# Moving the first batch's imaginary-part transfers, row tiles 0 and 1, from SyncE's DMA queue to GpSimd's

## The chip, the cores and the metric

The kernel runs on one core of a Trainium2 chip. The metric is the device time of one execution in microseconds (us), lower is better. The core has TensorE (PE, with its weight loads PEld), VectorE (DVE), ScalarE (ACT), GpSimd (POOL) and SyncE (SP). SP only issues transfers here; POOL issues transfers and does small copies. Transfers of either queue are carried by the same 16 DMA engines.

## The reference

Three stages follow each other. The first is a recurrence over time for 4 batches, 8 heads, 768 steps and a head width of 48; two MLP blocks work on its output.

```
S_re, S_im = 0
for t in range(S):
    new_re = ar * S_re - ai * S_im
    new_im = ar * S_im + ai * S_re
    S_re, S_im = new_re + k[t] v[t]^T, new_im
    y[t] = q[t] @ S_re
x = heads of y side by side              # B, S, 384
x = token mixing and channel MLP of x    # w_tok1, w_tok2, w_ch1, w_ch2
out = x + MLP(normalised x)              # g_ln, w_ch1, w_ch2
```

`ar` and `ai` are the complex decay, scaled to a magnitude of at most 0.999.

## The kernel before

The decay of a step is written as a magnitude and an angle, so that the recurrence becomes a product over time chunks of 128 steps: q and k are scaled by cumulated magnitudes and turned by cumulated angles. The turned vectors have a real part (times the cosine) and an imaginary part (times the sine). For one head both parts are stacked on 96 partitions of one tile, `stk`: rows 0 to 47 real, 48 to 95 imaginary. TensorE then works on a head with that one tile.

The elementwise work (generator `gen_E`, class `Piece`) does not go by heads. It goes by row tiles of 128 rows (head times width): a batch has 384 rows, so three row tiles i = 0, 1, 2, and in the first batch each is done in two halves `hf` of 384 time steps. Row tile 0 holds heads 0 and 1 and the first 32 rows of head 2; row tile 1 the last 16 rows of head 2, heads 3 and 4, and 16 rows of head 5; row tile 2 the rest. The steps of a piece are F, G (magnitudes and their cumulated product), H (scale q and k), T1, T2 (angles, sine, cosine) and T3.

T3 (line 318 on) does the product with the cosine into the piece's scratch `self.R` (DVE, line 173 is the helper that issues it) and the product with the sine in place into `qkt` (the tile `qk`). Then it copies, row range by row range, the real part (line 342, out of `t`, `u` or `w` in the profile's names, which are the scratch tiles) and the imaginary part (line 343, mostly out of `qk`) into the head's `stk`. In the first batch heads 2 to 7 use tiles with the tag `w2`, so the profile writes `w` for their `stk`. Row tile 0 gives 3 row ranges in each half, row tile 1 gives 4: 6 and 8 transfers of imaginary parts. The last real-part transfer of a row tile is kept as `fin["stk", i]`; the load of the next batch's decay (line 59, 768 KB) is issued after it.

TensorE's work on the heads is in `gen_P`: transposes of k (line 524), scores (line 538), filler matmuls `warm` (line 462), the chunk sums (line 566, which need `kT`, evacuated by ACT in line 526), a scan over the chunks on DVE (line 567), and the output (lines 586 and 598). DVE masks the scores (line 544).

The weights come as 64-bit words and are split on DVE and ACT (`split_w`, lines 632 to 648). `load_raw` (line 615) loads them: pieces 0 to 2 on SP's queue, the others on POOL's. POOL's queue also stores two split pieces early on (`tokw_d`, line 668).

The order of instructions is made in two steps. The Python code yields between generators by budgets (`run_E`, `run_P`, `run_W`), which gives the order in the program; then a planner built into the framework simulates a timeline and orders the instructions on each engine by which are ready first. On the chip each engine and each queue works strictly in that order and waits on semaphores.

`DQ` (line 1213) is empty in the kernel before, so the choice in line 343 always falls on SP:

```
last_dma = nc.sync.dma_start(out=stk[b, h][d0:d0 + m, hf], in_=self.R[r:r + m, k])
(nc.gpsimd if (b, i) in DQ else nc.sync).dma_start(out=stk[b, h][D + d0:D + d0 + m, hf], in_=qkt[r:r + m, k])
```

Of the kernel before, what the change touches and what calls it, by code (L numbers as in the profile page):

```python
# [17 lines left out]
B, H, S, D = 4, 8, 768, 48  # L18
# [4 lines left out]
FT = 1536 // P  # L23
# [15 lines left out]
def tile_kernel(ctx: ExitStack, tc: tile.TileContext, a_in, qk_in, v_in, aq2_in, v2_in, wt_in, wm1_in, wm2_in, w64_in, g_in, c_in, out):  # L39
# [41 lines left out]
    vstat = cp.tile([P, 2 * B], F32, name="vstat")  # L81
    n_q = 3 * len(YS) + 3 * len(QZ)
    qstat = cp.tile([P, max(n_q, 1)], F32, name="qstat")
# [28 lines left out]
    def tmp():  # L112
        return ap.tile([P, HB], F32, tag="r", name="r", bufs=NR)
# [42 lines left out]
    hscan = {}  # L156
# [29 lines left out]
    def after(key):  # L186
        return tc.issue_after(fin[key]) if key in fin else ExitStack()
# [15 lines left out]
    class Piece:  # L203
# [21 lines left out]
        def F(self):  # L225
# [4 lines left out]
            yield "wait"  # L230
            with tc.issue_after(tab["ops"][-1]) if b and GSQ else ExitStack():
                A.activation(out=self.sq.rearrange("p (x s) -> p x s", x=2), in_=self.both, func=AF.Square)  # L232
# [231 lines left out]
    def gen_P(alt):  # L464
# [22 lines left out]
        def evac(y, h, n):  # L487
            yv = y[:, 0:NCH * D].rearrange("p (c e) -> p c e", c=NCH)
            dst = slice(h * D, (h + 1) * D)
            scale = US / (VS * SS) if n in YS else US  # L490
            A.activation(out=xh[:, :, dst], in_=yv, func=AF.Copy, scale=scale)
            V.scalar_tensor_tensor(out=xl[:, :, dst], in0=yv, scalar=scale, in1=xh[:, :, dst], op0=ALU.mult, op1=ALU.subtract)
            A.activation(out=junk_p, in_=yv, func=AF.Square, scale=scale, accum_out=ustat[:, n:n + 1])

        for n, (b, h) in enumerate(heads):
# [3 lines left out]
            def qc(c, x):  # L499
                return kq[:, c // 3, x * HB + (c % 3) * P:x * HB + (c % 3 + 1) * P]  # L500
# [20 lines left out]
            for half in range(2):  # L521
                if half == 0:
                    for c in range(5):
                        T.transpose(tr[:, c * 96:(c + 1) * 96], qc(c, 1), eye[0:96, 0:96])  # L524
                    with after(AHOLD.get(n)):
                      kTc = A.activation(out=kT, in_=tr[:, 0:480].rearrange("p (c d) -> p c d", c=5), func=AF.Copy, scale=(VS * SS if n in YS else 1.0) / (QS if n in QZ else 1.0))
                    if n in YS:
                        vh = ap.tile([P, S], F32, tag="dw", name="vh", bufs=NDW).bitcast(F16)
                        Uh = vh[0:2 * D, 2 * NCH * D:4 * NCH * D].rearrange("p (x c e) -> p x c e", x=2, c=NCH)
                        Uc = U.rearrange("p e c -> p c e")  # L530
                        vh = vh[:, 0:2 * NCH * D].rearrange("p (x c e) -> p x c e", x=2, c=NCH)
                        m = YS.index(n)
                        A.activation(out=vh[:, 0], in_=v, func=AF.Copy, scale=VS)
# [3 lines left out]
                for c in range(3 * half, 3 * half + 3):  # L537
                    last = T.matmul(sc[:, (c % 3) * P:(c % 3 + 1) * P], qc(c, 1), qc(c, 0), start=True, stop=True)  # L538
                if n in YS or b == 0 and h % 2 < SR:
                    sT.append(tmp().rearrange("p (c t) -> p c t", c=3))  # L540
# [23 lines left out]
                if half == 1:  # L564
                    for c in range(5):
                        T.matmul(Gv.rearrange("p (e c) -> p e c", c=NCH)[:, :, c], kT[:, c], v[:, c], start=True, stop=True)  # L566
                    scan = V.tensor_tensor_scan(out=U.rearrange("p e c -> p (e c)"), data0=Gv, data1=dr.rearrange("p e c -> p (e c)"), initial=0.0, op0=ALU.add, op1=ALU.mult)
# [29 lines left out]
                elif c:  # L597
                    T.matmul(yc, qc(c, 0), U[:, :, c - 1], start=False, stop=True)
            late = (lambda y=y, h=h, n=n: evac(y, h, n))
            if h == H - 1 or not LATE:  # L600
                late()
                late = None
            yield ("done", b, h)
# [7 lines left out]
    def load_raw(n, tag):  # L611

        raw = ap.tile([P, 2, 2 * HB + 3], F32, tag="w2", name="raw", bufs=6).rearrange("p a b -> p (a b)")[:, 0:2 * S].bitcast(I32) if tag == "w2" else ap.tile([P, 2 * S], I32, tag="tw", name="raw", bufs=NTW)
        with after(("pc", 0, RG, 1) if RG >= 0 and 4 <= n < 6 else None):
          (nc.sync if n < NSY else nc.gpsimd).dma_start(out=raw.bitcast(U8), in_=w_src[n].bitcast(U8)[:, 3:3 + 8 * S])  # L615
        return raw

    def load_w(n):
        while len(raws) <= n:
            m = len(raws)  # L620
            raws[m] = load_raw(m, "w2" if m in RW2 else "tw")

    def split_w(dst, n):

        load_w(min(27, AHEAD(n)))
        if not pad:
            pad.append(ap.tile([P, S], U32, tag="pad", name="pad", bufs=1) if PADB else ap.tile([P, S], U32, tag="dw", name="pad", bufs=NDW))
            G.memset(pad[0], 0.0)
        raw = raws[n]
        byte = raw.bitcast(U8).rearrange("p (a b) -> p a b", b=8)[:, :, 4]  # L630
        y = raw.rearrange("p (a b) -> p a b", b=2)[:, :, 0]
        V.scalar_tensor_tensor(out=pad[0].bitcast(U8).rearrange("p (a b) -> p a b", b=4)[:, :, 3], in0=byte, scalar=3, in1=byte, op0=ALU.logical_shift_left, op1=ALU.bitwise_and)  # L632
        V.scalar_tensor_tensor(out=y.bitcast(U32), in0=y.bitcast(U32), scalar=5, in1=pad[0], op0=ALU.logical_shift_right, op1=ALU.bitwise_or)
        w = y.bitcast(F32).rearrange("p (i s) -> p i s", i=2)
        wact[n] = A.activation(out=dst[:, :, 0], in_=w, func=AF.Copy, scale=WS).ins
        if NW0 <= n < NW1:
            if not eye_w:
                eye_w.append(ap.tile([P, P], F32, name="eye_w"))
                eye_w.append(ap.tile([P, P], F16, name="eye_m"))
                A.activation(out=eye_w[0], in_=eye, func=AF.Copy, scale=WS)  # L640
                A.activation(out=eye_w[1], in_=eye, func=AF.Copy, scale=-1.0)
            for i in range(2):
                p = psum("y", 1)[:, 0:HB]
                T.matmul(p, eye_w[0], w[:, i], start=True, stop=False)
                T.matmul(p, eye_w[1], dst[:, i, 0], start=False, stop=True)
                A.activation(out=dst[:, i, 1], in_=p, func=AF.Copy)
            return
        wop[n] = V.scalar_tensor_tensor(out=dst[:, :, 1], in0=w, scalar=WS, in1=dst[:, :, 0], op0=ALU.mult, op1=ALU.subtract).ins
# [14 lines left out]
    def gen_W():  # L663
        for n in range(4):
            hl = wm1[STG + n]
            with after("scan"):
                split_w(hl, n)
            nc.gpsimd.dma_start(out=tokw_d[n // 2, :, n % 2], in_=hl)
            yield 0
        for j, wm in enumerate((wm1, wm2)):  # L670
            for n in range(FT):
                if j and n % 2 == 0:
                    w = ap.tile([P, 2, 2 * HB + 3], F32, tag="w2", name="w2", bufs=6).rearrange("p a b -> p (a b)")
                    for i in range(2):
                        wm2[n + i] = w[:, i * 2 * DM:(i + 1) * 2 * DM].bitcast(F16).rearrange("p (a b c) -> p a b c", a=2, b=2)
                with (tc.issue_after(hscan[WGH]) if 4 + j * FT + n >= WGN and j == 0 else after('r1') if 4 + j * FT + n >= WGR and j == 0 else ExitStack()):
                    split_w(wm[n], 4 + j * FT + n)
                yield j * FT + n + 1

# [364 lines left out]

    st = {"phase": "", "alt": True, "e": 0, "p": 0, "pp": 0, "w": 0, "need": 0, "bb": 0, "c": 0, "mk": 0}
    E, Pg, Wg, M = gen_E(), gen_P(lambda: st["alt"]), gen_W(), gen_M()

    e0 = []
# [69 lines left out]
    def check_next():  # L1118
        n = st["c"]
        if n >= 2:  # L1120
            check_w(n - 2)
        if n < 28:
            again[n] = load_raw(n, "tw")
        st["c"] += 1
# [20 lines left out]
    for b in range(B):  # L1145
        k = 0
        st["bb"] = b
        while True:
# [21 lines left out]
            for _ in range(2):  # L1170
                n = st["p"]
# [34 lines left out]
LATE = 1  # L1206
# [6 lines left out]
DQ = ()  # L1213
# [3 lines left out]
FE = 0  # L1217
LQ = 0
RG = -1
GSQ = 1  # L1220
PIPE = 0
IV = 0
WGN, WGR, WGH = 99, 99, 7
# [43 lines left out]
EW = 2  # L1267
LQ = 1
RG = 1
YS = [n for n in range(32) if n >= YH or n in YX]  # L1270
QZ = [n for n in range(32) if n >= QH or n in YX]
_INS = ["a", "qk", "v", "aq2", "v2", "wt", "wm1", "wm2", "w64", "g", "c"]
# [49 lines left out]
```

## Time and profile before

| | us |
|---|---|
| median of 3 runs | 899.06 |
| lowest, highest | 897.23, 906.02 |
| the profiled execution | 897.11 |
| its span, first to last instruction | 895.0 |
| PE busy (share of the span) | 802.0 (90%) |
| DVE, ACT, POOL busy | 630.4, 603.4, 93.5 |

The profiled execution is 2.1 us longer than its span. Times in the rows below count from the start of the span. A timeline row gives start, duration, engine, line, operation, output and inputs, and, in square brackets, how long the engine had been idle and what released it. "SPq" is SP's queue; the duration there is the time of issuing. A transfer lands later; the views of transfers give the time from issue to landing.

### The profile page before, as it was taken

What the parts mean: (1) busy time and instruction counts of PE and PEld (TensorE: products, weight loads), DVE (VectorE), ACT (ScalarE), POOL (GpSimd) and SP (SyncE); (2) the same over time, 40 slices, a digit from 0 to 9 for tenths busy, and PEclk for the clock granted to TensorE, in tenths of its full rate; (3) what the DMA queues carried; (4) which work ended last, traced back from release to release, by engine and by line L of the source; (5) the groups of instructions that cost most, each with busy time, mean ns of one, the idle gap of its engine ahead of it and who ended that gap; (6) DMA issues with size and microseconds to landing.
All of it is one profiled execution on the core that took longest, in us unless ns stands there. A gap on an engine that the chain in (4) does not pass through costs nothing.

```text
span 895.0 us, 15729 instructions
## 1 busy us (share of the span) xinstructions
PE 802.0 (90%) x5802; PEld 543.0 (61%) x5802; DVE 630.4 (70%) x1094; ACT 603.4 (67%) x1631; POOL 93.5 (10%) x171
## 2 busy tenths in 40 slices
PE   0089898999989898899999999999999999999996
PEld 0078785555757676456766666566666656656563
DVE  6797469999988799776898885956565332455443
ACT  8787248675668798984999984985665423454542
POOL 0311010311001010210030010100000000011110
PEclk9977979999999999999999999999999999999998
DMA  8355684255742715410421614131010111566662
GB/s 306 86 163 156 200 298 141 57 156 168 227 140 61 208 53 172 136 55 27 116 74 34 173 39 131 45 83 34 12 50 21 34 63 37 174 205 187 201 218 96
DMA packets 41604, 108.26 MB, mean 121 GB/s; under 512 B 5904, under 2 KB 23824, under 8 KB 41520
## 3 DMA queue, kind: packets, MB, share of 16 engines
q1 hardware_dynamic: 31936, 56.72, 21.3%
q0 software_dynamic: 9584, 50.47, 17.1%
q8 instruction: 47, 0.77, 0.4%
q14 instruction: 37, 0.30, 0.1%
HBM read 77.20 MB, written 11.01 MB: 99 GB/s over the span
## 4 chain that ended last, share of the span: by engine, by line
PE 44%; ACT 8%; DVE 5%; DMA 2%; issue 0%; SPq 0%; DVEq 0%; ACTq 0%
PE m L683 13%; PE m L682 13%; PE m L684 13%; ACT t L200 2%; DMA stk<-t 1%; PE sc L538 1%; ACT hid L690 1%; PE tr L566 1%; DVE t L173 1%; DVE hid L692 1%; ACT junk L745 0%; DVE xc L800 0%; DVE qk L173 0%; PE tr L817 0%; PE tr L524 0%
## 5 line engine op out<-in xcount | busy, mean ns | idle before, releaser
L692 DVE SCALAR_TENSOR_TENSOR hid<-m,hid 128x384 f16<-128x384 f32 x198 | 109.2, 553 | 131.9 <-ACT hid L690 131.5
L682 PE MATMUL m<-u,w 128*128 128x384 f16 x576 | 187.7, 326 | 6.4 <-DVE u L742 3.2
L684 PE MATMUL m<-u,w 128*128 128x384 f16 x576 | 187.7, 326 | 0.0
L683 PE MATMUL m<-u,w 128*128 128x384 f16 x576 | 187.7, 326 | 0.0
L683 PE MATMUL m<-hid,w 128*128 128x384 f16 x540 | 175.6, 326 | 4.8 <-DVE hid L692 4.5
L684 PE MATMUL m<-hid,w 128*128 128x384 f16 x540 | 175.5, 326 | 0.0
L690 ACT ACTIVATE hid<-m 128x384 f16<-128x384 f32 x198 | 95.3, 481 | 118.5 <-PE m L684 117.8
L684 PEld LDWEIGHTS <-w 128*128 128x128 f16 x1176 | 115.1, 98 | 81.9 <-issue 12.2
L683 PEld LDWEIGHTS <-w 128*128 128x128 f16 x1176 | 115.4, 98 | 79.0 <-issue 8.7
L682 PEld LDWEIGHTS <-w 128*128 128x128 f16 x1176 | 114.5, 98 | 79.2 <-issue 12.5
L682 PE MATMUL m<-hid,w 128*128 128x384 f16 x540 | 128.9, 326 | 9.3 <-ACT hid L690 9.2
L173 DVE SCALAR_TENSOR_TENSOR t<-t 128x384 f32<-128x384 f32 x80 | 44.2, 554 | 21.5 <-ACT t L232 14.0
L538 PE MATMUL sc<-stk 96*128 96x128 f32 x300 | 44.3, 282 | 1.4 <-DVE r L544 1.4
L661 ACT ACTIVATE sq<-sq 128x768 f16<-128x768 uint8 x28 | 23.6, 843 | 28.3 <-DVE sq L660 28.3
L615 POOL DMA_DIRECT2D raw<-in_wm x48 | 25.6, 534 | 162.0 <-DVE sq L660 83.0
L538 PEld LDWEIGHTS sc<-stk 96*128 96x128 f32 x300 | 40.0, 194 | 3.7 <-DVE r L544 1.7
L200 ACT ACTIVATE t<-t 128x384 f32<-128x384 f32 x80 | 40.9, 514 | 0.5 <-DVE t L173 0.3
L524 PE MATMUL m<-cst,stk 96*128 96x96 f32 x10 | 1.7, 291 | 43.2 <-DMA stk<-qk 43.2
L690 ACT ACTIVATION_READ_ACCUMULATOR hid<-m 128x1 f32 x198 | 38.6, 195 | 0.0
L173 DVE TENSOR_TENSOR qk<-qk,t 128x768 f32<-128x768 f32 x40 | 38.0, 951 | 0.4
L198 ACT ACT_TABLE_LOAD x27 | 34.6, 1283 | 1.3 <-PEq L1314 0.9
L632 DVE SCALAR_TENSOR_TENSOR pad<-raw 128x768 uint8<-128x768 uint8 x28 | 28.8, 1029 | 9.0 <-DMA raw<-in_wt 6.1
(281 smaller groups left out, 1689.0 us busy)
## 6 DMA issues: line engine op xcount, KB each, us to landing
raw<-in_wm POOLq DMA_DIRECT2D x48, 768.0 KB, 4.9
qk<-in_qk SPq DMA_DIRECT2D x23, 384.0 KB, 4.0
aj<-in_a SPq DMA_DIRECT2D x9, 768.0 KB, 5.0
stk<-t SPq DMA_DIRECT2D x40, 144.6 KB, 3.1
stk<-qk SPq DMA_DIRECT2D x40, 144.6 KB, 3.1
raw<-in_wt SPq DMA_DIRECT2D x6, 768.0 KB, 5.9
v<-in_v SPq DMA_DIRECT2D x32, 144.0 KB, 2.3
x_d<-xc SPq DMA_DIRECT2D x24, 192.0 KB, 2.8
```

Source lines behind the costliest of these rows:

```text
L173: r = getattr(nc.vector, n)(*a, **k)
L198: tab.update(set=s, load=A.preload_act_table_set(sets[s]).ins, ops=[])
L200: tab["ops"].append(A.activation(**k).ins)
L538: last = T.matmul(sc[:, (c % 3) * P:(c % 3 + 1) * P], qc(c, 1), qc(c, 0), start=True, stop=True)
L615: (nc.sync if n < NSY else nc.gpsimd).dma_start(out=raw.bitcast(U8), in_=w_src[n].bitcast(U8)[:, 3:3 + 8 * S])
L632: V.scalar_tensor_tensor(out=pad[0].bitcast(U8).rearrange("p (a b) -> p a b", b=4)[:, :, 3], in0=byte, scalar=3, in1=byte, op0=ALU.logical ...
L661: A.activation(out=t[:, HB:2 * HB].bitcast(F16), in_=bad_, func=AF.Copy, accum_out=wstat[:, n:n + 1])
L682: T.matmul(out_, wh, xh_, start=first, stop=False)
L683: T.matmul(out_, wh, xl_, start=False, stop=False)
L684: T.matmul(out_, wl, xh_, start=False, stop=last)
L690: A.activation(out=hl[:, 0], in_=p, func=AF.Relu, accum_out=hstat[:, n_h[0]:n_h[0] + 1])
L692: last[:] = [V.scalar_tensor_tensor(out=hl[:, 1], in0=p, scalar=0.0, in1=hl[:, 0], op0=ALU.max, op1=ALU.subtract).ins]
```

## The change

`DQ` becomes `((0,0),(0,1))`: in batch 0, the imaginary-part transfers of row tiles 0 and 1 (14 transfers) are issued from GpSimd's queue. Real parts, row tile 2 and the batches 1 to 3 stay on SP.

The diff also adds three names whose values leave the rest as it was: `EV` is empty, `WH` is empty (so `WH.get(n, "scan")` is `"scan"`), and `RGN` is `(4, 5)`, which is the old `4 <= n < 6`.

```diff
-            if h == H - 1 or not LATE:
+            if h == H - 1 or not LATE or n in EV:
...
-        with after(("pc", 0, RG, 1) if RG >= 0 and 4 <= n < 6 else None):
+        with after(("pc", 0, RG, 1) if RG >= 0 and n in RGN else None):
...
-            with after("scan"):
+            with after(WH.get(n, "scan")):
...
-                with (tc.issue_after(hscan[WGH]) if 4 + j * FT + n >= WGN and j == 0 else after('r1') if 4 + j * FT + n >= WGR and j == 0 else ExitStack()):
+                with after(WH[4 + n]) if j == 0 and 4 + n in WH else (tc.issue_after(hscan[WGH]) if 4 + j * FT + n >= WGN and j == 0 else after('r1') if 4 + j * FT + n >= WGR and j == 0 else ExitStack()):
...
+RGN = (4, 5)
+WH = {}
+EV = ()
...
+DQ = ((0,0),(0,1))
```

## Rows read from the trace of the kernel before

**Rows 1.** The page: span and the first engine's busy time.
```profile
span 895.0 us, 15729 instructions
...
PE 802.0 (90%) x5802; PEld 543.0 (61%) x5802; DVE 630.4 (70%) x1094; ACT 603.4 (67%) x1631; POOL 93.5 (10%) x171
```

**Rows 2.** Timeline of PE, 30 to 130 us.
```profile
43.18 0.71 PE L524 MATMUL m<-cst,stk 96*128 96x96 f32 x3 [43.18 <-DMA stk<-qk]
...
51.31 1.05 PE L566 MATMUL m<-v,kT 128*96 128x48 f32 x10 [1.78 <-ACT kT L526]
...
66.79 0.67 PE L524 MATMUL m<-cst,w 96*128 96x96 f32 x3 [1.15 <-issue]
```

**Rows 3.** Timeline of SP's queue, 0 to 130 us.
```profile
39.93 1.16 SPq L343 DMA_DIRECT2D stk<-qk  x2
...
64.28 2.42 SPq L343 DMA_DIRECT2D w<-qk  x4
...
71.19 0.59 SPq L343 DMA_DIRECT2D w<-qk  x1
...
95.47 0.63 SPq L615 DMA_DIRECT2D raw<-in_wt  x1
```

**Rows 4.** Transfers issued at 39.93 and at 64.28: count, KB, us to landing.
```profile
stk<-qk SPq DMA_DIRECT2D x1, 144.6 KB, 3.1
...
w<-qk SPq DMA_DIRECT2D x1, 48.2 KB, 2.4
```

**Rows 5.** Waits of PE, 0 to 160 us: total us, times, longest us.
```profile
PE m L598 <- DVE U L567: 2.9, 2, 2.2
```

**Rows 6.** Timeline of DVE, 18 to 75 us.
```profile
31.53 0.95 DVE L648 SCALAR_TENSOR_TENSOR w<-raw,w 128x768 f16<-128x768 f32 x1
...
38.24 0.95 DVE L173 TENSOR_TENSOR qk<-qk,t 128x768 f32<-128x768 f32 x1
...
40.83 0.96 DVE L173 TENSOR_TENSOR qk<-qk,t 128x768 f32<-128x768 f32 x1
45.27 0.56 DVE L544 TENSOR_TENSOR r<-sc,cst 128x384 f32<-128x384 f32 x1 [3.48 <-PE sc L538]
...
49.25 0.56 DVE L173 SCALAR_TENSOR_TENSOR u<-aj,u 128x384 f32<-128x384 f32 x1
...
62.91 0.95 DVE L173 TENSOR_TENSOR qk<-qk,u 128x768 f32<-128x768 f32 x1
...
64.76 0.96 DVE L173 TENSOR_TENSOR qk<-qk,w 128x768 f32<-128x768 f32 x1
68.83 0.56 DVE L544 TENSOR_TENSOR r<-sc,cst 128x384 f32<-128x384 f32 x1 [3.11 <-PE sc L538]
```

**Rows 7.** Timeline of ACT, 18 to 75 us.
```profile
48.71 0.51 ACT L270 ACTIVATE u<-u 128x384 f32<-128x384 f32 x1
...
50.71 0.55 ACT L526 ACTIVATE kT<-m 128x480 f32<-128x480 f32 x1
```

**Rows 8.** Lines L668 and L615 alone: durations in ns, min/median/max, and landing in us.
```profile
DMA to landing us min/median/max: 2.6/2.7/5.8
...
L615 POOL DMA_DIRECT2D raw<-in_wm x48: 528/528/562, 52.7 to 873.7; - x48
```

**Rows 9.** Timeline of POOL, 0 to 120 us.
```profile
27.32 2.98 POOL L324 COPY t<-pstat 128x3 f32<-128x3 f32 x1
...
32.78 0.56 POOL L668 DMA_DIRECT2D tokw_d<-w  x1 [1.17 <-DVE w L648]
...
48.25 0.10 POOL L329 MEMSET qk<- 128x1 f32 x1 [13.32 <-DVE aj L173]
...
70.87 0.19 POOL L278 TENSOR_TENSOR pstat<-aj,w 128x3 f32<-128x3 f32 x1 [16.77 <-DVE w L173]
```

**Rows 10.** Waits of DVE, 90 to 130 us.
```profile
DVE pad L632 <- DMA raw<-in_wt: 6.1, 1, 6.1
```

## The prediction

> **What bounds the kernel now.** I read the page first: PE is busy for 802.0 of 895.0 us [rows 1], so 93 us are idle, and an early change can only buy some of those. The timeline of PE says where nearly half of them lie: 43.18 us come before the first matmul, and what ends them is a transfer of imaginary parts, `stk<-qk` [rows 2]. That is one of the 14 transfers of this change. The second place is 66.79, where the first transposes of head 2 begin after 1.15 us of idle PE [rows 2]; the profile has no clear releaser ("issue"), but the transfer of head 2's imaginary part, issued at 64.28 and 2.4 us under way, lands at 66.7 [rows 3, 4], so this is it. The waits of PE up to 160 us add no other such transfer of any length; the largest of the rest is 2.9 us, in two pieces, on a scan of DVE [rows 5]. After that the views of the timeline have to say whether a gain at either place is passed on; for that I followed DVE and ACT from 38 to 75 us [rows 6, 7].
>
> **What the change does, step by step.** 6 transfers of row tile 0 and 8 of row tile 1 leave SP's queue. An issue takes some 0.58 us on SP (1.16 us for two at 39.93) [rows 3] and 0.53 us on POOL [rows 8], so SP is rid of 14 x 0.58 = 8.1 us of issuing and POOL gets 14 x 0.55 = 7.7 us. POOL has room: it is idle for 13.32 us up to 48.25 and for 16.77 us up to 70.87 [rows 9], and both groups fall into these holes. Nothing is queued behind them there that anybody waits for.
>
> *Tile 0, first half.* The sine product ends at 38.24 + 0.95 = 39.19 [rows 6]. SP begins its transfer only at 39.93, since real parts stand ahead of it [rows 3]. POOL would begin sooner, but not at once: in the one place where POOL issues a transfer right after a DVE result, DVE ends at 31.53 + 0.95 = 32.48 and POOL starts at 32.78, 0.30 later [rows 6, 9]. So 39.49, or 0.44 us earlier. The time to landing is 3.1 us from SP [rows 4]; a transfer of this size from POOL isn't in the trace. Bounds: POOL's stores of 384 KB land in 2.6 to 5.8 us [rows 8]; the fast end would be 0.5 us better than SP's, the slow end 2.7 us worse. I take 3.1, as on SP, because both go through the same engines and the smallest, least disturbed row is the nearest one. PE then starts at 43.18 - 0.44 = 42.7.
>
> *Does it carry on?* DVE sits idle for 3.48 us until the first scores come [rows 6] and would go on 0.44 us sooner, at 44.83. It works without a hole up to 49.25, where it needs ACT's result of 48.71 + 0.51 = 49.22 [rows 6, 7]. ACT is in an unbroken run there and had waited for none of these transfers. PE for its part waits at 51.31 for `kT` from ACT, 50.71 + 0.55 = 51.26 [rows 2, 7], which stands in the same run. So the 0.44 us turn into a longer wait on ACT: worth 0.
>
> *Tile 0, second half.* The sine product ends at 41.79 [rows 6] and the last transfer of these goes out a few us sooner. Nobody waits for it: PE's next wait is the one on `kT`. 0.
>
> *Tile 1, first half.* The sine product ends at 62.91 + 0.95 = 63.86 [rows 6]. POOL would start at 64.16, SP started at 64.28 [rows 3]: 0.12 us. With its landing time [rows 4] PE starts at 66.67 instead of 66.79 and DVE's first mask, which ends an idle time of 3.11 us [rows 6], moves as much. DVE is then busy without a hole for several us, so here a gain is passed on. Bounds as above: 0.5 us better to 2.7 us worse in the landing. I take -0.1.
>
> *Tile 1, second half.* Product done at 64.76 + 0.96 = 65.72. POOL is through with the first four at 64.16 + 4 x 0.55 = 66.4 and issues the next four by 68.6; on SP the last started at 71.19 [rows 3]. That is up to 3 us earlier, but PE has no wait in this stretch that such a transfer ends (its waits there are on DVE's scan [rows 5]), so 0. SP, free earlier, starts the next batch's 768 KB decay load earlier; it then shares the engines with the last imaginary parts. Their 3 us of head start covers that; without the cover a load of that size on the path would cost some 2 us.
>
> A page of the Trainium skill speaks against the change: "SBUF — State Buffer", in the warning on DVE blocking DMA, says that a transfer issued from GpSimd has its descriptors written by GpSimd, which cannot write them while DVE holds the port that the two share. The trace shows such a thing for a copy: 2.98 us for 3 columns at 27.32, with DVE busy all along [rows 9]. It does not show it for a transfer: 48 issues on POOL took 528 to 562 ns, although DVE is busy 70% of the time [rows 1, 8], and the fastest store landed in 2.6 us. By the rule the sum would be the slower rival below, by the rows it is the forecast.
>
> **Sum.** 0 + 0 - 0.1 + 0 = -0.1 us on the profiled execution's 897.11 us, so 897.0. The median of the runs shown is 899.06, 2 us above it, and the lowest 897.23; I stay with 897.0, as two of the four times known lie there.
>
> **Rivals.**
>
> *Slower: POOL's transfers are held up by DVE.* The place is where DVE does two products right behind the one that released POOL. In tile 0 DVE is busy until 41.79; if descriptors wait for that, the transfer lands at 41.8 + 2.6 = 44.4 instead of 43.05, PE starts 1.3 us later, and DVE's run from 45.27 to 49.25 has no slack to take it up. In tile 1 DVE is busy to 65.72, against an issue at 64.28: 1.4 us more. Sum +2.7, so 899.8; twice that, 902.5, if the landing goes to the slow end. It decides from a landing 0.44 us slower in tile 0 or 0.12 us in tile 1. For it: the 2.98 us copy [rows 9]; against it: the short, even issues and the 2.6 us landing [rows 8].
>
> *Faster: the planner puts the weight load earlier.* DVE waits 6.1 us for the weight piece that SP issues at 95.47 behind everything else [rows 3, 10]. The planner orders each queue by simulated readiness, and a simulated SP with 8 us less work, heads done sooner, may issue that load before row tile 2's transfers. DVE's 6.1 us would then be filled with splitting, the time 897.1 - 6.1 = 891; with PE's waits on the scan of DVE, which stand behind it, gone as well (2.9 us [rows 5]), 888. For it: SP's queue is where the change takes work away. Against: row tile 2's transfers stay on SP, and the load stays behind them in the program.
>
> *The planner's order changes for the worse*, a weight load of 768 KB falling on the transfers of a row tile: as much as the 6.1 us [rows 10] once or twice, 903 to 909.
>
> *It does nothing at all*: no row says that an SP wait was long; the result is then 897 to 899 and can't be told from the forecast.
>
> **How the numbers follow.** The forecast (with "nothing") 0.54, POOL held up 0.16, load earlier 0.21, a worse order 0.09. About 1%, 9 us, is what a measurement of this kernel can tell from no change, as its own runs spread over 8.8 us. Faster by more (below 890): most of the third case, 0.19. Slower by more (above 908): 0.04 from the slow end of the second case and 0.07 of the fourth, 0.11. Within: 0.70. The range: down to 888 for the third case, up to 904 for the second; the forecast's own range is 895 to 900.
>
> **What would show it.** Right: `stk<-qk` and the early `w<-qk` on POOL at about 39.5 and 64.2 with landings of 2.4 to 3.1 us; PE's first matmul at 42.7, the wait for `kT` longer by as much, and the matmul of 51.31 where it was; PE's head 2 within 0.3 us of 66.79. Wrong: POOL's transfers issued or landed after 41.8 and 65.7 (held up), the weight load of 95.47 at another place (new order), or the stage from 130 us on shifted by more than 1 us.

## The result and the profile after

| | before | after |
|---|---|---|
| median, us | 897.7 (894.83 to 906.02, 20 runs) | 905.39 (901.4 to 911.25, 20 runs) |
| ratio to before, 95% interval | | 1.0075 [1.0056, 1.0094] |
| span of the profiled execution, us | 895.0 | 906.3 |

The change costs 0.75%, some 7 us, and the interval lies wholly above 1. The forecast was no change (897.0, range 888 to 904).

The page of the kernel after, first and third line of its first part, against [rows 1]:

```profile
span 906.3 us, 15749 instructions
...
PE 807.6 (89%) x5802; PEld 541.4 (60%) x5802; DVE 632.0 (70%) x1094; ACT 603.2 (67%) x1631; POOL 103.8 (11%) x185
```

TensorE does the same 5802 matmuls, but is busy 5.6 us longer with them. POOL has the 14 transfers more. DVE and ACT do the same work. So half of the 11.3 us by which the spans differ is not idle time of TensorE; that is a first hint.

**The transfers themselves.** Timeline of POOL after, then timeline of DVE after (`qk<-qk` are the sine products that release the transfers; the row at 40.77 is a cosine product beside them, and the last two rows are for later):

```profile
40.42 1.06 POOL L343 DMA_DIRECT2D stk<-qk  x2 [4.56 <-DVE qk L173]
41.47 0.50 POOL L343 DMA_DIRECT2D w<-qk  x1
43.30 1.00 POOL L343 DMA_DIRECT2D stk<-qk  x2 [1.32 <-DVE qk L173]
...
65.56 4.15 POOL L343 DMA_DIRECT2D w<-qk  x8 [5.22 <-DVE qk L173]
```

```profile
39.18 0.95 DVE L173 TENSOR_TENSOR qk<-qk,t 128x768 f32<-128x768 f32 x1
40.77 0.96 DVE L173 TENSOR_TENSOR t<-qk,t 128x768 f32<-128x768 f32 x1 [0.64 <-ACT t L200]
41.77 0.96 DVE L173 TENSOR_TENSOR qk<-qk,t 128x768 f32<-128x768 f32 x1
...
64.33 0.95 DVE L173 TENSOR_TENSOR qk<-qk,u 128x768 f32<-128x768 f32 x1
...
66.18 0.96 DVE L173 TENSOR_TENSOR qk<-qk,w 128x768 f32<-128x768 f32 x1
...
77.55 0.53 DVE L544 TENSOR_TENSOR r<-m,cst 128x384 f32<-128x384 f32 x1
...
81.35 0.74 DVE L567 TENSOR_TENSOR_SCAN U<-m,dr 96x288 f32<-96x288 f32 x1
```

The whole execution stands 0.94 us later than that of before even ahead of the change (39.18 against 38.24 [rows 6]); that much is to be taken off each time up to here. POOL starts 0.29 us after the first product (40.42 against 40.13) and 0.28 us after that of row tile 1 (65.56 against 65.28), but 0.57 us after the second product of row tile 0 (43.30 against 42.73), which the runs don't explain. An issue takes 0.50 to 0.53 us, also where DVE is busy beside it, as at 41.47, across the end of its product of 40.77 and the start of the next. The views of transfers of POOL, issued from 40.3 to 41 us and from 65.4 to 66.2 us (count, KB, median us to landing):

```profile
stk<-qk POOLq DMA_DIRECT2D x2, 144.6 KB, 3.7
...
w<-qk POOLq DMA_DIRECT2D x1, 48.2 KB, 2.6
```

They land in 3.7 and 2.6 us, against 3.1 and 2.4 for transfers of the same sizes on SP [rows 4]. And this is what TensorE makes of it, in its timeline after:

```profile
44.19 0.71 PE L524 MATMUL m<-cst,stk 96*128 96x96 f32 x3 [44.19 <-DMA stk<-qk]
...
68.29 0.71 PE L524 MATMUL m<-cst,w 96*128 96x96 f32 x3 [1.98 <-issue]
...
82.15 0.66 PE L598 MATMUL m<-U,w 96*128 96x48 f32 x2 [5.81 <-DVE U L567]
...
137.34 0.32 PE L682 MATMUL m<-w,hid 128*128 128x384 f16 x1 [1.95 <-DVE u L742]
...
184.78 0.32 PE L682 MATMUL sc<-hid,w 128*128 128x384 f16 x1 [1.56 <-ACT hid L690]
...
223.18 0.32 PE L682 MATMUL sc<-hid,w 128*128 128x384 f16 x1 [2.37 <-ACT hid L690]
```

The first row, less 0.94, is 43.25 against 43.18 [rows 2]: what POOL's earlier start gives, its slower landing takes. The second row stands 3.01 us behind the end of the product that it needs (68.29 against 65.28); in the kernel before it was 2.93 us (66.79 against 63.86 [rows 2, 6]).

**The order.** From here on the rows don't answer to those of before one by one, because the planner made another order. Counted in the program's instructions, TensorE's first 104 and DVE's first 97 are alike; behind them 1072 of TensorE's places, 428 of DVE's and 440 of ACT's hold another instruction, and from some 415 us on all three are alike again. The row at 82.15 shows it well: before, head 2's mask and scan stood ahead of row tile 2's elementwise work; the timeline of DVE before has

```profile
72.41 0.55 DVE L544 TENSOR_TENSOR r<-m,cst 128x384 f32<-128x384 f32 x1
...
75.08 0.72 DVE L567 TENSOR_TENSOR_SCAN U<-m,dr 96x288 f32<-96x288 f32 x1
```

and after they stand at 77.55 and 81.35, behind that work, and TensorE waits 5.81 us. The weight load of [rows 3] moved too, from 95.47 to 91.12, still behind row tile 2's transfers (timeline of SP's queue after), and DVE's wait of [rows 10] for it shrank from 6.1 to 3.3 us (waits of DVE after, 85 to 130 us):

```profile
89.27 0.60 SPq L343 DMA_DIRECT2D w<-u  x1
89.91 0.61 SPq L59 DMA_DIRECT2D aj<-in_a  x1
91.12 0.35 SPq L615 DMA_DIRECT2D raw<-in_wt  x1
```

```profile
DVE pad L632 <- DMA raw<-in_wt: 3.3, 1, 3.3
```

**Where the time is lost.** I cut the span at three places that both orders share: TensorE's first matmul, the first ACTIVATE of L690 (the first hidden units that `relu_split` makes) and the 61st, in the second batch. The table of stretches, each with length, busy time and count of the engines, granted clock of TensorE, share and rate of DMA, for the head stage and for the first batch's MLP stage; before, then after:

```profile
43.18:141.11 97.93, 86.48 (x611) 75.23 (x612) 68.93 (x109) 56.50 (x134) 13.47 (x29) 0.83 0.64 202
141.11:400.17 259.06, 236.53 (x1701) 158.61 (x1700) 230.57 (x378) 206.60 (x536) 36.33 (x61) 1.00 0.43 131
```

```profile
44.19:143.51 99.32, 82.93 (x612) 70.60 (x613) 79.98 (x122) 59.01 (x139) 24.72 (x41) 0.86 0.67 218
143.51:411.17 267.66, 245.62 (x1700) 161.69 (x1699) 222.20 (x366) 203.78 (x533) 34.06 (x62) 0.96 0.41 120
```

Read the third busy time, DVE's: 68.93 became 79.98 in the head stage and 230.57 became 222.20 behind it. The new order does some 11 us of weight splitting earlier. The head stage is 1.4 us longer and the MLP stage 8.6. What follows to the end is alike to 0.3 us (468.7 and 469.0 us to the 193rd ACTIVATE, then 26.1 in both). In the MLP stage TensorE waits no longer than before (22.0 us in all, against 22.5), but its granted clock is 0.96 instead of 1.00: 20.5 us at the lower level, 1.2 GHz. They begin 1.1 us after the wait that ends at 184.78, 0.3 us after that of 223.18, and at 349.8; one more such stretch, 0.8 us after the wait of 137.34, still counts with the head stage.

### The profile page after: what moved, and what is told of

The parts are those of the page before. It is cut to its first block, busy times and chain, and to the rows that moved or that the text cites. A ratio compares the mean times of both kernels' runs of the same rounds, so it can differ in the third digit from the quotient of the medians.

```text
span 906.3 us, 15749 instructions
## 1 busy us (share of the span) xinstructions
PE 807.6 (89%) x5802; PEld 541.4 (60%) x5802; DVE 632.0 (70%) x1094; ACT 603.2 (67%) x1631; POOL 103.8 (11%) x185
## 4 chain that ended last, share of the span: by engine, by line
PE 47%; ACT 12%; DVE 11%; DMA 3%; SPq 2%; issue 1%; POOL 0%; DVEq 0%; ACTq 0%; POOLq 0%
PE m L682 14%; PE m L683 13%; PE m L684 13%; ACT t L200 3%; DVE t L173 2%; DMA stk<-t 2%; PE sc L538 2%; SPq L343 1%; DVE qk L173 1%; DVE hid L692 1%; DMA stk<-qk 1%; PE tr L566 1%; ACT hid L690 1%; SPq L342 1%; ACT L198 1%
## 5 line engine op out<-in xcount | busy, mean ns | idle before, releaser
L690 ACT ACTIVATE hid<-m 128x384 f16<-128x384 f32 x198 | 95.5, 483 | 119.4 <-PE m L684 118.9
L615 POOL DMA_DIRECT2D raw<-in_wm x48 | 25.8, 537 | 145.8 <-DVE sq L660 87.3
L690 ACT ACTIVATION_READ_ACCUMULATOR hid<-m 128x1 f32 x198 | 38.7, 195 | 0.0
L635 ACT ACTIVATE w<-raw 128x768 f16<-128x768 f32 x28 | 25.3, 904 | 17.5 <-DVE raw L633 17.4
L278 POOL TENSOR_TENSOR pstat<-aj,t 128x3 f32<-128x3 f32 x20 | 21.9, 1093 | 126.7 <-DVE t L173 93.3
```

Source lines behind the costliest of these rows:

```text
L278: fin["pc", self.b, self.i, self.hf] = (nc.vector if ACP else nc.gpsimd).tensor_tensor(out=pc, in0=n_end, in1=w_end, op=ALU.mult).ins
L690: A.activation(out=hl[:, 0], in_=p, func=AF.Relu, accum_out=hstat[:, n_h[0]:n_h[0] + 1])
```

## The experiments

Theories at the start: *order theory*, the planner's new order costs the time wherever the transfers go; *queue theory*, the transfers on POOL cost it. To hold an order, the kernel hands the framework, just before the block ends, the order of another kernel for every engine, as edges without a semaphore (`pin`; the order stands in the kernel as a packed table, and `FREE` is empty). Each ratio below is to runs of the kernel before taken beside that experiment, whose medians were 896.45 to 898.25 us.

**All four corners: e1 to e4.** e1 has the 14 transfers on POOL and the order of before; e2 has them on SP and the new order. The 14 transfers themselves are in neither table.

```diff
+    pin(tc)
     main.close()
...
+def pin(tc):
...
+    table = json.loads(zlib.decompress(base64.b85decode(ORDER)))
+    here = {i.name: i for i in tc.nc.cur_bb.bb.instructions}
+    for engine, ids in table.items():
+        row = [here[f"I-{n}"] for n in ids if f"I-{n}" in here and f"I-{n}" not in FREE]
+        for a, b in zip(row, row[1:]):
...
+            tc.add_manual_dep(b, a.name, mybir.DependencyInfo(mybir.DependencyClass.NoSync, mybir.DependencyReason.DATA), reason="pin")
```

> All 14 transfers on POOL as in the changed kernel, but every engine's order pinned to that of the kernel before. Two theories of the 0.75% (7 us) that the change costs. Order theory: the planner laid out the rest of the program differently (from about 72 us on), and that order costs the time; then this kernel is within 2 us of before, ratio 0.998 to 1.002. Queue theory: the transfers themselves are worse from POOL (later landings, collisions with SP's earlier loads); then it keeps the loss, ratio 1.006 to 1.009.

> The other half of the square: all transfers on SP as before, every engine's order pinned to that of the changed kernel. Order theory: the loss is there without any transfer on POOL, ratio 1.006 to 1.010. Queue theory: within 2 us of before, 0.998 to 1.002.

e3 and e4 leave the planner free and move one row tile each:

```diff
-DQ = ((0,0),(0,1))
+DQ = ((0,0),)
```

```diff
-DQ = ((0,0),(0,1))
+DQ = ((0,1),)
```

> Only row tile 0's six transfers on POOL, planner free. The planner leaves the order of PE, DVE and the queues as before here (two instructions of ACT change places). Order theory: within 2 us of before. Queue theory: about 6 of 14 of the loss, ratio 1.003 to 1.004.

> Only row tile 1's eight transfers on POOL, planner free. The planner makes the same order of PE, DVE and the queues as in the changed kernel. Order theory: the whole loss, ratio 1.006 to 1.010. Queue theory: about 8 of 14 of it, ratio 1.004 to 1.005.

| | transfers on POOL | order | median, us | ratio [95%] |
|---|---|---|---|---|
| e1 | both row tiles | before | 896.39 | 0.998 [0.9954, 1.0005] |
| e2 | none | after | 905.78 | 1.008 [1.005, 1.0111] |
| e3 | row tile 0 | before but for a few neighbouring places on ACT | 898.85 | 1.0007 [0.9987, 1.0027] |
| e4 | row tile 1 | after but for the same places on ACT | 904.68 | 1.0074 [1.0045, 1.0104] |

The order decides, the queue does not: with the transfers on SP and the new order the whole loss is there; with them on POOL and the old order none of it. Moving row tile 1 is enough to make the planner change its order, moving row tile 0 is not. e2 has the wait, too (timeline of its TensorE):

```profile
80.20 0.66 PE L598 MATMUL m<-U,w 96*128 96x48 f32 x2 [6.00 <-DVE U L567]
```

**Which half of the new order: e5 and e6.** Both have the transfers on POOL. e5 has the new order up to the first MLP product (some 141 us) and then the rest in the old order, e6 the other way round; only the table handed to `pin` is another. For TensorE, DVE, ACT and SP e5's is what this line gives (it doesn't stand in the kernel, which holds the finished table):

```
table = {e: new_prefix[e] + [n for n in old[e] if n not in new_prefix[e]] for e in old}
```

> The 14 transfers on GpSimd's queue, every engine's order pinned: the planner's new order up to the first product of the first MLP (about 141 us), the order of before behind it. Two theories of where the new order costs its 7 us. Head theory: in the head stage of the first batch, where DVE's U scan of head 2 (L567) stands behind row tile 2's elementwise chain and TensorE idles 5.8 us: 903 to 907 us here, ratio about 1.007. MLP theory: in the first MLP, where the new order leaves short idle times on TensorE that are each followed by a stretch at the half clock: 896 to 899 us here, ratio 0.998 to 1.001.

> The other half: the 14 transfers on GpSimd's queue, the order of before up to the first product of the first MLP, the new order behind it. Head theory: 896 to 899 us, ratio 0.998 to 1.001. MLP theory: 903 to 907 us, ratio about 1.007, with stretches at the half clock between 130 and 400 us. If both halves cost something, e5 and e6 lie each 2 to 5 us above the kernel with all of the old order (896.4) and their excesses add up to about 9 us.

Measured: 911.29 us, 1.0156 [1.0107, 1.0205], and 922.8 us, 1.0271 [1.022, 1.0322]. Both are worse than either whole order, which neither theory had allowed. The rows point to the joint: work that one order does early and the other late is missing on one side of it. In e6 TensorE stands for 10.93 us just behind the joint (timeline):

```profile
151.74 0.48 PE L682 MATMUL m<-u,w 128*128 128x384 f16 x1 [10.93 <-DVE u L742]
```

and in e5 it waits for sums of the second MLP block's normalisation (L817) and for a mean of them (L798) that come late (waits, 120 to 400 us):

```profile
PE tr L817 <- DVE r L816: 6.2, 1, 6.2
...
PE sc L798 <- DVE sT L544: 3.2, 1, 3.2
```

So these two runs don't tell the halves apart.

**Is it the wait at 82 us: e7 and e9.** Both have the new order with some head instructions put back ahead of row tile 2's work. e7 moves head 2's mask (its text says norm multiply) and scan on DVE; e9 moves besides them head 3's masks, scan and `xl`, and head 3's `kT` on ACT. On TensorE, DVE, ACT and SP their finished tables are what these lines make of the new order (`mv(row, x, a)` moves instruction x behind a; the second is applied on top of the first):

```
mv(table["DVE"], 718, 738); mv(table["DVE"], 724, 808)
```

```
for x, a in ((797, 911), (821, 797), (827, 821), (799, 827)): mv(table["DVE"], x, a)
mv(table["Activation"], 791, 671)
```

> The new order everywhere, but for two DVE instructions: head 2's norm multiply (L544) and its U scan (L567) are put back ahead of row tile 2's elementwise chain, as they stood before. Head theory: TensorE's wait of 5.8 us at L598 shrinks to under 2 us and the time falls by 3 to 6 us, to 900 to 902. MLP theory: the wait shrinks too, but the gain is used up by the first MLP, 904 to 906 us.

> The changed kernel with the planner's new order everywhere, but for seven instructions that are put back ahead of row tile 2's elementwise chain: on DVE head 2's mask and U scan (718, 724) and head 3's masks, U scan and xl (797, 821, 827, 799), on ACT head 3's kT (L526). Head theory (half or more of the loss is made before the first L690, where heads 2 and 3 stand behind row tile 2): TensorE's waits of 5.8 us at 82 and of 4.7 us for kT go to under 1.5 us each, the stage from the first matmul to the first L690 falls from 99.4 to 94 to 96 us, and the time by 3 to 5 us, to 900 to 902. If what is put back only makes row tile 2 late, the stage stays at 99 us or above and the time at 904 to 906, as in e7.

e7: 905.34 us, 1.011 [1.0059, 1.0161]. The wait of 5.8 us is gone (0.82 us are left), the gain is not there. TensorE's timeline shows what stands in its place: the next late thing is `kT`, which ACT has behind the same row tile's work.

```profile
84.81 1.83 PE L566 MATMUL m<-v,kT 128*96 128x48 f32 x10 [4.72 <-ACT kT L526]
```

e9 puts that back as well and is slower, not faster: 915.98 us, 1.0204 [1.0165, 1.0244]. Now row tile 2 itself is late, and the heads that need it (waits of TensorE in e9, 44 to 150 us):

```profile
PE tr L683 <- DVE xl L492: 6.9, 1, 6.9
PE m L524 <- DMA w<-w: 4.2, 1, 4.2
```

The gains that the head theory named are not there. e7 and e9 don't price the wait by themselves, since other waits took its place. Two of the runs below do: e12 and e13, with the planner free, have next to nothing of it and are as slow as the changed kernel. In e12 the waits of TensorE on that scan come to 2.0 us, in e13 none reaches the list (waits, 44 to 140 us; e12):

```profile
PE m L598 <- DVE U L567: 2.0, 2, 1.3
```

So the largest wait of the new order is not its price.

**Is it the clock: e8, e10 and e11.** They have the new order and put matmuls that add zeros ahead of waiting products, 40 in e8, 15 in e10; e11 is e9 and e10 together. In e8 the first ten did not fill their wait but stood in it themselves (waits of TensorE in e8, 130 to 400 us; L1511 is the line of the added matmuls):

```profile
PE m L1511 <- DVE u L742: 1.8, 1, 1.8
```

```diff
-        T.matmul(out_, wh, xh_, start=first, stop=False)
+        fill(tc, bias, eye_h, out_, first); T.matmul(out_, wh, xh_, start=first, stop=False)
...
+FILL_AT = {1387: 10, 1955: 8, 2488: 13, 4006: 9}
...
+def fill(tc, bias, eye_h, out_, first):
+    zero = bias[:, 3:4].bitcast(F16)[:, 0:1].to_broadcast([P, HB])
+    for _ in range(FILL_AT.get(int(tc.nc.cur_bb.bb.instructions[-1].name[2:]) - len(FILLER), 0)):
+        FILLER.append(int(tc.nc.tensor.matmul(out_, eye_h, zero, start=first, stop=first).ins.name[2:]))
```

In e10 the line of `FILL_AT` is

```diff
+FILL_AT = {1955: 4, 2488: 6, 4006: 5}
```

> The changed kernel with every engine's order as the planner made it, and 40 matmuls more that add zeros, in front of four waits of TensorE in the first MLP (10 ahead of the first product, the one that waits at 137.3 us, 8 and 13 ahead of the two that wait for ACT's hid at 184.8 and 223.2, 9 ahead of the one that waits at 352.1). Each takes about 0.16 us and they lie in waits of 1.6 to 2.4 us. Clock theory (the part of the loss behind 141 us is the half-clock stretches that begin at these waits): no half clock between 130 and 400 us, the stage from the first to the 121st L690 on ACT falls from 255 to 262 us to about 251, and the time by 4 to 6 us, to 900 to 902. Rival (the half clock comes from elsewhere or costs nothing, the stage is longer because of the order of the work itself): that stage stays above 255 us, and the time is the changed kernel's 905 or, with the 40 matmuls' 6.4 us, up to 3 us more.

> As e8, but with 15 instead of 40 of the matmuls that add zeros: 4 and 6 ahead of the two that wait at 184.8 and 223.2 us, 5 ahead of the one at 352.1, none at 137.3; together 2.5 us at the full clock, in waits of 5.6 us. Clock theory: the half clock behind those three waits (17 us in the changed kernel's profile) is under 4 us, the stage from the first to the 121st L690 is 251 to 254 us, and the time 901 to 903. Rival: the stage stays at 255 us or above, the time at 905 to 907.

> The edits of e9 and of e10 together. If both theories hold, the two parts add up: 897 to 899 us, ratio 0.998 to 1.002, the kernel before with the planner's new order otherwise in place. If only one holds 901 to 903, if none does 905 to 908.

The "121st L690" of these texts counted accumulator reads and queue entries as well; the cut at the 61st ACTIVATE, used here, lies some 6 to 8 us later, so that 251 there is 259 here. By the cut of the texts the stage is 257.1 us in both e8 and e10. e8: 907.54 us, 1.0104 [1.0069, 1.0139]. e10: 903.54 us, 1.0072 [1.0048, 1.0096]. e11: 916.03 us, 1.0206 [1.0163, 1.0248], as e9. In e10 the clock does stay up at the places filled (table of stretches, 180 to 200 and 220 to 240 us):

```profile
180.00:200.00 20.00, 17.77 (x107) 10.28 (x106) 17.25 (x29) 14.39 (x39) 1.78 (x5) 1.00 0.68 200
220.00:240.00 20.00, 19.16 (x127) 12.60 (x127) 19.86 (x32) 15.99 (x32) 1.58 (x3) 1.00 0.63 200
```

where the changed kernel had 0.91 and 0.83. Yet 6.8 us at the lower level turn up at 311 and 359 us, the MLP stage is 262.97 us, and the time is that of the changed kernel within its interval. The 2 to 4 us that the clock theory named for e10 aren't shown; a gain of 2 us, about the length of the added matmuls, can't be excluded.

**One flaw, or another draw: e12 to e14.** The planner is free in all three. e12 leaves of row tile 1 only head 2's transfers on POOL, e13 leaves all but these, e14 is the changed kernel with one edge that puts head 2's mask back ahead of the product before it.

```diff
+                    (nc.gpsimd if (b, i) in DQ and (i == 0 or h == 2) else nc.sync).dma_start(out=stk[b, h][D + d0:D + d0 + m, hf], in_=qkt[r:r + m, k])
```

```diff
+                    (nc.gpsimd if (b, i) in DQ and (i == 0 or h > 2) else nc.sync).dma_start(out=stk[b, h][D + d0:D + d0 + m, hf], in_=qkt[r:r + m, k])
```

```diff
+HINT = [(718, 769)]
...
+    for x, y in HINT:
+        tc.add_manual_dep(here[f"I-{y}"], f"I-{x}", mybir.DependencyInfo(mybir.DependencyClass.NoSync, mybir.DependencyReason.DATA), reason="hint")
```

> As the changed kernel, but of row tile 1 only head 2's two imaginary-part transfers go to GpSimd's queue; the other six stay on SyncE's. The planner is free, and its order is a third one: it parts from the order of before at TensorE's 94th matmul and differs from that of the changed kernel at about a tenth of the places. Draw theory (any small edit in row tile 1 makes the planner draw another order, the order of before is a good draw, and the others lie 3 to 15 us above it): 900 to 912 us. Late-head theory (the planner plans badly only because it takes head 2's transfers on GpSimd's queue for late): 904 to 907 us, the same as the changed kernel.

> The opposite choice: of row tile 1, head 2's two transfers stay on SyncE's queue and those of heads 3, 4 and 5 go to GpSimd's; the planner is free. Late-head theory: head 2 is where it was, so the time is that of before, 896 to 899 us. Draw theory: 900 to 912 us, and close to e12, whose order it shares nearly everywhere.

> The changed kernel, planner free, with one added edge: on DVE head 2's second mask (L544) is to stand ahead of the product that the new order puts before it, as in the order of before. The planner makes the rest anew. Draw theory: another draw, anywhere from 897 to 915 us. If the place of this mask is what costs the time: 897 to 900 us.

Measured: 905.59 us, 1.0082 [1.0055, 1.011]; 904.97, 1.0072 [1.0047, 1.0097]; 904.69, 1.0072 [1.0048, 1.0096]. The late-head theory falls with e13, which has head 2 on SP and is as slow. So does the idea that the place of that mask costs the time (e14). All three times lie in the draw theory's range, but they are too alike for free draws, and the orders in the profiles, where TensorE has 5802 matmuls, say why: e14's differs from the changed kernel's only between TensorE's 193rd and 411th matmul, and e12's and e13's (equal on TensorE and DVE) only ahead of the 410th and behind the 2018th. The stretch between, 114 to 367 us of the changed kernel and so most of the first batch's MLPs, all have in common with the changed kernel, while the order of before differs there at 876 of 1607 places. e13's table of stretches:

```profile
43.73:141.50 97.77, 85.44 (x612) 73.05 (x613) 79.64 (x122) 59.24 (x138) 21.29 (x39) 0.84 0.71 221
141.50:407.68 266.18, 243.20 (x1700) 162.02 (x1699) 222.16 (x366) 203.97 (x533) 35.16 (x62) 0.97 0.41 121
```

Its head stage is as short as that of the kernel before (97.77 against 97.93) and its MLP stage as long as that of the kernel after.

**All profiles together.** Us of each stage and, in it, of TensorE at the lower clock level; in the MLP stage TensorE's idle time as well. One profiled execution each, so single values scatter (e2's profile was shorter than its median by some 6 us).

| | head | low | MLP | low | idle |
|---|---|---|---|---|---|
| before | 97.9 | 34.1 | 259.1 | 0 | 22.5 |
| e1 | 94.2 | 23.9 | 259.2 | 6.8 | 19.5 |
| e3 | 94.4 | 23.9 | 260.7 | 0 | 24.1 |
| after | 99.3 | 27.3 | 267.7 | 20.5 | 22.0 |
| e2 | 99.4 | 30.7 | 260.7 | 6.8 | 20.5 |
| e4 | 99.5 | 34.1 | 262.5 | 13.7 | 20.2 |
| e12 | 99.7 | 37.5 | 266.7 | 17.1 | 21.8 |
| e13 | 97.8 | 30.7 | 266.2 | 13.7 | 23.0 |
| e14 | 99.9 | 30.7 | 263.6 | 10.2 | 22.5 |

The first three are of the old order, the other six of new ones. Means: head 95.5 and 99.3, MLP 259.6 and 264.5: 3.8 and 4.9 us, 8.7 together, against 6 to 8 by the medians. In the MLP stage the idle time is the same (22.0 and 21.7) and the time at the lower level is 2.3 and 13.7 us. At half the rate (in after 0.16 us from one product to the next behind 137.34, 0.32 us behind 139.14), 11.4 us more of it are worth up to 5.7 us, which is the size of the excess there. In the head stage, too, the time at the lower level is longer in the new orders, 31.8 against 27.3 us.

That the clock is the cause is not shown, and the results of all runs, which give the span and the mean granted clock of each, speak against it for most of the loss. 114 runs of the old order (before, e1, e3) have a mean clock of 0.976 and a mean span of 896.1 us, 71 of the new ones (after, e2, e4, e12, e13, e14) 0.972 and 903.4 us. The nine profiles overstate the difference of the clocks (0.980 against 0.972). And runs of the same clock still differ: at 0.975 the mean span is 896.6 us in 13 runs of the old order and 901.9 in 8 of the new ones, at 0.972 it is 897.3 in 6 and 902.9 in 11. A straight line through each group, with one slope for both, leaves 5.5 of the 7.3 us between them at equal clock, so that the clock goes along with some 1.8 us. e10 says the same: its 12 runs have the clock of the runs of the kernel before beside it (0.977 in both) and are 6.4 us longer, of which the added matmuls can be 2.5.

## Why the prediction was wrong

**The bound.** Right that the first 43 us end with a transfer of this change: in the kernel after it is one too (44.19, released by `stk<-qk`). Whether a gain there would be passed on was not tested, since there was none.

**Start, landing, row tile 0.** POOL's start 0.30 us after DVE: measured 0.29 and 0.28 for the two that were priced. The landing of 3.1 us taken from SP was mis-sized: 3.7 us for the first pair (again 3.7 in e1 and e3), inside the bounds of 2.6 to 5.8. So TensorE started no sooner and the step "ACT takes up the 0.44 us" was never put to the test. That the sum of row tile 0 came out as 0 (e3 gives 1.0007) is therefore luck in part: a slower landing, not a longer wait on ACT, used up the earlier start.

**"POOL held up by DVE".** The landings were 0.6 and 0.2 us slower than on SP, more than the 0.44 and 0.12 us at which the prediction let this rival decide; why, the runs don't show. But the times that it gave did not come. It counted a landing 2.6 us behind the end of DVE's second product (42.73 and 67.14 here); the transfers landed at 44.1 and 68.2, only 1.4 and 1.1 us behind it. And e1, with all 14 transfers on POOL, is at 0.998. The sign that was to tell it ("landed after 41.8 and 65.7") could not: the forecast's own landings, 42.6 and 66.6, lie behind these times. The warning of the Trainium skill's "SBUF — State Buffer" on DVE blocking DMA describes another DVE operation (a copy in a two-port mode), a condition that the prediction had left out; beside the 128x768 f32 products here the issue at 41.47 took 0.50 us and the landings came as just said.

**Row tile 1, "-0.1": the step that failed.** It priced the eight transfers by what waits for them on the chip and left every other instruction where it was. On the chip the term was near: 3.01 us from the product to TensorE's start against 2.93, so +0.1 instead of -0.1. But the transfers are also an input of the planner, and that the sum put at nothing: moving these eight alone (e4) brings the new order and 1.0074, while all 14 with the order held (e1) are at 0.998. I had the planner in the prediction, but as two rivals about one weight load on SP: issued ahead of row tile 2's transfers, with a gain of up to 9 us and a chance of 0.21, or falling on a row tile's transfers, with a loss of 6 to 12 us and 0.09. Neither is what happened. The load did move, from 95.47 to 91.12, and DVE waits 2.8 us less for it, but it still stands behind row tile 2's transfers, and the time went up. The same order puts 11 us of weight splitting ahead of the first MLP and heads 2 and 3 behind row tile 2; what became of the 2.8 us the runs don't show. The second rival's price was near the mark; its mechanism is not what the runs show, and its chance was too small.

**Smaller readings.** POOL's 14 issues took 7.2 us, not 7.7 (the sum took 0.55 us each where the rows have 0.53). Of the 2.9 us on DVE's scan that the rival for 888 counts behind the weight load, 0.69 us stand ahead of it, at 75.85. The 2 us for a decay load on the path had no row behind them and were not in the sum.

**The observation that was named for it.** "The stage from 130 us on shifted by more than 1 us" and the weight load "at another place (new order)" were the right signs to look for: the first batch's MLP stage is 1 to 8 us longer in the profiles of the new orders than the mean of the old ones, and the load moved.

**What stays open.** That the new order costs the time is shown (e1, e2). Which decision in it does is not: the wait at 82 us isn't the price (e12, e13), the head stage has some 4 us of the loss but e13, with 2 of them in its profile, is as slow, and TensorE's lower clock goes along with some 1.8 of the 7.3 us. What the slow kernels have in common is the order of the stretch from 114 to 367 us; no run has that stretch alone.

## What to carry to other kernels

Where a planner orders the instructions, an edit of one DMA queue is an edit of all engines' orders: compare the orders before and after first, and price the edit alone by holding the old order (here 0.998 instead of 1.0075). The largest wait that a new order shows need not be its price; e7 removed it and got another in its place, and e12 and e13 were as slow without it. And orders can't be joined at will: halves of the two, joined at one place, were 1.6% and 2.7% slower than the kernel before.

## What the chip did that I had not expected

TensorE's clock fell from 2.4 to 1.2 GHz behind waits of 1.6 to 2.4 us in the middle of dense work, and not in every execution: the wait of 2.37 us for `hid`, which after has at 223.18, stands at 218.53 in e2 with the same order,

```profile
218.53 0.32 PE L682 MATMUL sc<-hid,w 128*128 128x384 f16 x1 [2.37 <-ACT hid L690]
```

and there the clock stayed up, as it did in the kernel before behind this one:

```profile
259.00 0.65 PE L682 MATMUL m<-hid,w 128*128 128x384 f16 x3 [2.40 <-ACT hid L690]
```

Two profiles of one and the same order lie 8 us apart (spans of 906.3 in after and 897.9 in e2), 7.0 us of it in the MLP stage, where they have 20.5 and 6.8 us at the lower level. So a stage is to be compared over several profiles.
